# Delta-rule recurrence: multiplying by Z chunk by chunk instead of ahead of the loop

## The chip, the cores and the metric

The kernel runs on one core of a Trainium2 chip. A core has five engines with a queue each: TensorE (PE in the profile, with PEld for its weight loads), VectorE (DVE), ScalarE (ACT), GpSimd (POOL) and SyncE (SP). They work in parallel and wait for each other through semaphores. The metric is the device time of one execution in microseconds; the time given for a kernel is the median of its runs.

## What is computed

Two stages follow each other. The first is a recurrence over 768 tokens for 4 batches of 8 heads, with a state of 48 x 48 for each head; the second is a mixer over the 384 channels that the heads make together.

```python
k_n = k / (norm(k) + 1e-06)
for t in range(768):
    y[t]  = q[t] @ state
    v_old = k_n[t] @ state
    state = state + beta[t] * outer(k_n[t], v[t] - v_old)
x  = y of all heads, side by side                     # (4, 768, 384)
u  = x + (x.T @ U @ V).T                              # rank 32
out = u + relu(u @ w_ch1) @ w_ch2                     # 384 -> 1536 -> 384
```

## The kernel before

**Chunks.** The recurrence is not run token by token. The 768 tokens of a batch are cut into 12 chunks of 64 (`L`). Within a chunk the dependence of each token on those ahead of it is a triangular matrix, and the kernel inverts it, so that a chunk is a handful of products. Call the inverse Z, the keys of the chunk K, the (scaled) values v and the state ahead of the chunk S. What a chunk adds is z = Z v - (Z K) S; its outputs are the queries times S plus a masked product of queries and keys times z; the new state is S + K' z.

**Units.** Half a batch, six chunks, is a unit: units 0 and 1 belong to batch 0, units 2 and 3 to batch 1, and so on to unit 7. `grams` forms the products of keys and of queries and keys (L700), `norms` and `blocks` scale and invert (a long row of small DVE operations at L803 and L809, then joins of blocks on TensorE at L860, L874, L900, L903, L918 and L921, with ACT copies at L908, L927 and L939). The inverse of a unit lies in a region named `pg` or `zt`. The regions of two units alternate (`slot0`, `slot1`); the loads of unit n wait until the recurrence is through with unit n - 2 (L525).

**What is made ahead.** `prepare` (L1014) runs once for each half of a unit, three chunks. It makes Z K for all heads (24 products of 64 x 64, L1023) and Z v (24 products, L1034). Two ACT copies bring them back: Z K over the keys' region (L1042, 128 x 768 elements), Z v over the values (L1047, 128 x 576). It issues no DMA.

**The recurrence.** `recur` (L1055) has one turn for each chunk c. Step b multiplies Z K by the state (8 small products, L1072). A DVE operation subtracts that from Z v and gives z (L1085). Step s multiplies K by z (8 products, L1100) and a DVE operation adds it to the state (L1111). `outputs` (L975) makes the outputs in two steps of 8 products, y1 from the state (L983) and y2 from z (L997), and two ACT copies put them into `X` (L967). So the state goes round through two TensorE steps and two DVE operations in each chunk. Everything else in a chunk hangs beside that ring.

**The mixer.** When all chunks of a batch are done, `front` makes the low-rank part (L1393, L1412) and turns the result around (L1436). `wide` multiplies by `w_ch1` (L1497, ReLU on ACT at L1462) and `w_ch2` (L1617, gathered into `X` by DVE at L1537). The last batch uses another scheme for the first of these (L1296). The mixer of batch b runs while the recurrence of batch b + 1 does; that of the last batch has nothing beside it. The weights are converted by DVE and ACT operations at L1198, L1212, L1219 and L1226 in the first 150 us.

**Shapes on TensorE.** Mixer products use the whole array of 128 x 128 (L1497, L1617, L1436, L1296, and the transposes at L672). Those of the recurrence use it as four quarters of 64 x 64, and the joins at L900 to L921 as sixteen parts of 32 x 32.

**The order.** Every piece of work is a Python generator that yields what it does next. The string `ORDER` (L144 on) is a list written out in full: it says for each of some 2,260 steps which generator goes on. All engines' queues follow from it, and nothing reorders at run time; an engine waits at the head of its queue. Psum banks are taken in pairs: four pairs at first, three from the start of the mixer on.

Of the kernel before, what the change touches and what calls it, by code (L numbers as in the profile page):

```python
# [27 lines left out]
def kernel(  # L28
# [20 lines left out]
    nc = tc.nc  # L49
# [64 lines left out]
    def need(*keys):  # L114
        return [key for key in keys if key[1] >= 0]
# [29 lines left out]
    add_up b0 i0 f00: 573 585 613; add_up b0 i0 f03: 645 676 690; add_up b0 i1 f00: 795 797 800; add_up b0 i1 f03:  # L145
    818 819 824; add_up b0 i2 f00: 942 944 1042; add_up b0 i2 f03: 1023 1051 1071; add_up b1 i0 f00: 1161 1166 1186;
    add_up b1 i0 f03: 1189 1190 1191; add_up b1 i1 f00: 1309 1337 1363; add_up b1 i1 f03: 1357 1359 1368; add_up b1
    i2 f00: 1488 1493 1571; add_up b1 i2 f03: 1564 1572 1576; add_up b2 i0 f00: 1695 1717 1737; add_up b2 i0 f03:
    1728 1729 1730; add_up b2 i1 f00: 1888 1895 1906; add_up b2 i1 f03: 1886 1889 1901; add_up b2 i2 f00: 1992 2000
    2026; add_up b2 i2 f03: 2046 2047 2049; add_up b3 i0 f00: 2185 2186 2188; add_up b3 i0 f03: 2191 2192 2195;  # L150
    add_up b3 i1 f00: 2201 2202 2207; add_up b3 i1 f03: 2208 2209 2210; add_up b3 i2 f00: 2227 2228 2236; add_up b3
    i2 f03: 2224 2225 2229; blocks n0: 61 73 75 76 82 84 86 88 89 91 93 94 96 97 103 110 114 122; blocks n1: 143 157
    160 163 173 175 179 192 201 206 208 212 213 215 218 219 226 229; blocks n2: 479 496 501 502 508 512 513 514 515
    516 518 519 525 532 534 536 539 542; blocks n3: 704 720 721 729 730 733 739 741 761 765 769 771 772 773 778 779
    780 781 783 785 786 787 791 798 801 802 813 815 823 828 829 834 836 838; blocks n4: 971 982 985 987 989 996 1007
    1009 1012 1036 1038 1039 1040 1064 1074 1077 1082 1083 1087 1090 1107 1116 1119 1120 1122 1127 1129 1131 1132
    1133 1137 1138 1139 1140; blocks n5: 1168 1195 1198 1207 1218 1225 1227 1230 1231 1236 1241 1244 1249 1259 1269
    1271 1276 1278 1281 1286 1288 1291 1293 1294 1298 1311 1313 1314 1316 1323 1324 1332 1333 1351; blocks n6: 1510
    1523 1532 1541 1547 1558 1563 1566 1567 1568 1569 1596 1603 1612 1616 1617 1620 1622 1624 1645 1649 1653 1660
    1663 1665 1666 1671 1672 1673 1674 1675 1681 1684 1699; blocks n7: 1713 1724 1725 1739 1741 1744 1757 1762 1767  # L160
    1773 1775 1780 1782 1783 1800 1806 1807 1810 1817 1824 1829 1834 1837 1838 1849 1850 1856 1857 1860 1865 1866
    1867 1879 1881; both f0: 2149; both f1: 2105; both f2: 2147; both f3: 2123; both f4: 2111; both f5: 2184;
    channels b0 i0 e0: 546 547; channels b0 i0 e1: 549 550; channels b0 i0 e2: 552 553; channels b0 i0 e3: 567 574;
    channels b0 i0 e4: 588 591; channels b0 i0 e5: 604 633; channels b0 i1 e0: 768 776; channels b0 i1 e1: 777 788;
    channels b0 i1 e2: 790 792; channels b0 i1 e3: 799 803; channels b0 i1 e4: 806 807; channels b0 i1 e5: 808 814;
    channels b0 i2 e0: 898 899; channels b0 i2 e1: 907 912; channels b0 i2 e2: 935 936; channels b0 i2 e3: 950 959;
    channels b0 i2 e4: 965 969; channels b0 i2 e5: 995 1005; channels b1 i0 e0: 1118 1130; channels b1 i0 e1: 1136
    1148; channels b1 i0 e2: 1150 1151; channels b1 i0 e3: 1153 1155; channels b1 i0 e4: 1156 1158; channels b1 i0
    e5: 1159 1175; channels b1 i1 e0: 1297 1299; channels b1 i1 e1: 1300 1302; channels b1 i1 e2: 1304 1305; channels
    b1 i1 e3: 1306 1307; channels b1 i1 e4: 1326 1327; channels b1 i1 e5: 1342 1343; channels b1 i2 e0: 1430 1431;  # L170
    channels b1 i2 e1: 1432 1449; channels b1 i2 e2: 1450 1469; channels b1 i2 e3: 1470 1497; channels b1 i2 e4: 1498
    1501; channels b1 i2 e5: 1516 1530; channels b2 i0 e0: 1650 1654; channels b2 i0 e1: 1656 1669; channels b2 i0
    e2: 1686 1687; channels b2 i0 e3: 1689 1692; channels b2 i0 e4: 1697 1698; channels b2 i0 e5: 1700 1701; channels
    b2 i1 e0: 1808 1812; channels b2 i1 e1: 1813 1831; channels b2 i1 e2: 1833 1841; channels b2 i1 e3: 1843 1869;
    channels b2 i1 e4: 1871 1873; channels b2 i1 e5: 1874 1876; channels b2 i2 e0: 1950 1959; channels b2 i2 e1: 1960
    1961; channels b2 i2 e2: 1973 1979; channels b2 i2 e3: 1987 1999; channels b2 i2 e4: 2011 2027; channels b2 i2
    e5: 2033 2037; copies f0: 2127 2136; copies f1: 2082 2095; copies f2: 2129 2142; copies f3: 2086 2107; copies f4:
    2085 2103; copies f5: 2166 2168; cut f0 k0 to0: 2173; cut f0 k0 to1: 2169; cut f0 k1 to1: 2152; cut f1 k0 to0:
    2139; cut f1 k0 to1: 2106; cut f1 k1 to1: 2112; cut f2 k0 to0: 2153; cut f2 k0 to1: 2158; cut f2 k1 to1: 2163;
    cut f3 k0 to0: 2146; cut f3 k0 to1: 2154; cut f3 k1 to1: 2206; cut f4 k0 to0: 2171; cut f4 k0 to1: 2137; cut f4  # L180
    k1 to1: 2165; cut f5 k0 to0: 2181; cut f5 k0 to1: 2187; cut f5 k1 to1: 2194; diagonals n0 h0: 188 190 191 195 210
    222; diagonals n0 h1: 167 169 171 176 181 186; diagonals n1 h0: 312 315 319 336 343 353; diagonals n1 h1: 290 292
    303 338 349 358; diagonals n2 h0: 576 577 578 579 595 600; diagonals n2 h1: 632 646 665 670 705 707; diagonals n3
    h0: 854 855 860 865 870 873; diagonals n3 h1: 848 849 885 905 960 966; diagonals n4 h0: 1160 1162 1172 1197 1200
    1215; diagonals n4 h1: 1164 1192 1205 1211 1223 1226; diagonals n5 h0: 1356 1361 1365 1375 1402 1413; diagonals
    n5 h1: 1354 1380 1392 1419 1443 1444; diagonals n6 h0: 1708 1710 1711 1738 1745 1749; diagonals n6 h1: 1712 1723
    1726 1747 1753 1754; diagonals n7 h0: 1899 1905 1913 1931 1942 1945; diagonals n7 h1: 1892 1898 1911 1912 1918
    1957; first f0: 2160; first f1: 2097; first f2: 2135; first f3: 2138; first f4: 2092; first f5: 2180; front b0
    i0: 495 500 506 509 524 537; front b0 i1: 556 562 602 624; front b0 i2: 634 640 672 680; front b1 i0: 1055 1065
    1066 1078 1091 1111; front b1 i1: 1216 1224 1232 1237; front b1 i2: 1338 1348 1412 1425; front b2 i0: 1595 1599  # L190
    1605 1608 1623 1628; front b2 i1: 1633 1661 1702 1764; front b2 i2: 1801 1811 1835 1845; front b3 i0: 2041 2042
    2048 2050 2052 2054; front b3 i1: 2055 2061 2062 2067; front b3 i2: 2068 2070 2074 2076; gather b0 i0 h0 c0
    finalFalse: 671; gather b0 i0 h0 c0 finalTrue: 695; gather b0 i0 h0 c1 finalTrue: 756 1010; gather b0 i0 h1 c0
    finalFalse: 710; gather b0 i0 h1 c0 finalTrue: 757 805; gather b0 i0 h1 c1 finalFalse: 715; gather b0 i0 h1 c1
    finalTrue: 738; gather b0 i1 h0 c0 finalFalse: 820; gather b0 i1 h0 c0 finalTrue: 831; gather b0 i1 h0 c1
    finalTrue: 896 1061; gather b0 i1 h1 c0 finalFalse: 851; gather b0 i1 h1 c0 finalTrue: 881 1367; gather b0 i1 h1
    c1 finalFalse: 868; gather b0 i1 h1 c1 finalTrue: 867; gather b0 i2 h0 c0 finalFalse: 1017; gather b0 i2 h0 c0
    finalTrue: 1041; gather b0 i2 h0 c1 finalTrue: 1105 1185; gather b0 i2 h1 c0 finalFalse: 1079; gather b0 i2 h1 c0
    finalTrue: 1097 1163; gather b0 i2 h1 c1 finalFalse: 1084; gather b0 i2 h1 c1 finalTrue: 1086; gather b1 i0 h0 c0
    finalFalse: 1188; gather b1 i0 h0 c0 finalTrue: 1204; gather b1 i0 h0 c1 finalTrue: 1272 1778; gather b1 i0 h1 c0  # L200
    finalFalse: 1229; gather b1 i0 h1 c0 finalTrue: 1277 1591; gather b1 i0 h1 c1 finalFalse: 1238; gather b1 i0 h1
    c1 finalTrue: 1247; gather b1 i1 h0 c0 finalFalse: 1358; gather b1 i1 h0 c0 finalTrue: 1378; gather b1 i1 h0 c1
# [298 lines left out]

    TURNED = 3
    TURNED_K = 3
    SPLIT, QUARTERED = (0, 1), (2,)
    FIRST = dict(k1=11, q0=12, q1=13, z0=14, v0=15, z1=16, v1=17)
    FIRST = {(x[0], int(x[1])): y for x, y in FIRST.items()}

# [1188 lines left out]
```

## Time and profile before

| | |
|---|---|
| median of 3 runs | 599.51 us (597.67 to 601.25) |
| the profiled execution | 596.6 us, of which the profile's span is 594.9 us |
| DVE / ACT / POOL busy | 69% / 36% / 22% of the span |
| mean granted TensorE clock | 0.943 of full speed |
| Z K products, L1023 | 768 records, 16.8 us busy, last at 465.8 us |
| Z v products, L1034 | 768 records, 16.4 us busy, last at 466.7 us |
| step s, L1100 | 704 records, first at 61.0 us, last at 479.9 us |
| mixer, L1497 and L1617 | 150.1 us and, over three groups, 177.8 us busy |

A product is two records, since a 32-bit product is run as two instructions: a step of 8 products is "x16" in the trace and one of 24 is "x48". Lines of the trace give the start of a group, how long it lasted from the first start to the last end, the engine, the source line, what is written and read, and the shape; in brackets stands the idle time just before and who ended it. Groups on TensorE overlap, so the time that one takes from the next is read from start to start. In time, the program has four parts: until 60 us the first two units are loaded and inverted; until 108.5 us batch 0's recurrence runs, with no mixer work beside it; until 486 us the mixer of batches 0 to 2 and the recurrence of batches 1 to 3 share TensorE; the rest is the mixer of batch 3.

### The profile page before, as it was taken

The numbers are of one execution on the slowest core, as the hardware profiler recorded it, in microseconds if no ns is written. First come the engines' busy times: TensorE is split into PE (matmuls) and PEld (weight loads), VectorE is DVE, ScalarE is ACT, GpSimd is POOL, SyncE is SP. The second block draws the span as 40 slices with busy tenths as digits, with TensorE's granted clock in tenths as the row PEclk, the third lists the DMA queues.
The fourth block names the chain that finished last, engine by engine and source line by source line (L and its number), as shares of the span: only waits on it lengthen the run. The fifth ranks groups of instructions, "written<-read, shape, count | busy, mean of one in ns | idle before, by whom it ended". The sixth has DMA issues, their size and how long they took to land.

```text
span 594.9 us, 23426 instructions
## 1 busy us (share of the span) xinstructions
PE 559.7 (94%) x10428; PEld 481.6 (81%) x10428; DVE 409.3 (69%) x1011; ACT 216.8 (36%) x442; POOL 133.3 (22%) x229
## 2 busy tenths in 40 slices
PE   3778978899999999999999999999999999999997
PEld 3578977678988887989889887889899868656997
DVE  3888758899999458999884279998883235313542
ACT  1846475446322542035224341252243321335000
POOL 8122036116010724141205214520310000000000
PEclk9855556999999999999999999999999999999999
DMA  9981639714030415240402144420401000000000
GB/s 140 180 176 24 214 80 197 152 56 79 3 65 12 68 31 92 46 91 13 82 2 43 18 83 90 79 56 2 95 7 43 4 2 4 16 8 1 26 28 28
DMA packets 89445, 36.23 MB, mean 61 GB/s; under 512 B 75456, under 2 KB 87104, under 8 KB 89344
## 3 DMA queue, kind: packets, MB, share of 16 engines
q1 hardware_dynamic: 80800, 24.69, 20.7%
q0 software_dynamic: 6944, 9.74, 8.3%
q8 instruction: 82, 1.34, 1.0%
q10 hardware_dynamic: 1600, 0.30, 0.3%
q14 instruction: 19, 0.16, 0.1%
HBM read 29.98 MB, written 4.72 MB: 58 GB/s over the span
## 4 chain that ended last, share of the span: by engine, by line
PE 83%; DVE 11%; issue 2%; ACT 2%; DMA 1%; SPq 0%; DVEq 0%; ACTq 0%
PE P L1617 27%; PE P L1497 22%; PE P L1296 7%; PE P L700 4%; DVE xt L809 3%; DVE prod L803 3%; PE P L1072 2%; PE P L860 2%; PE P L874 2%; PE P L1023 2%; PE P L1034 2%; PE P L983 2%; PE P L997 2%; PE P L1100 2%; PE P L1412 2%
## 5 line engine op out<-in xcount | busy, mean ns | idle before, releaser
L1497 PE MATMUL P<-ut,w_sb 128*128 128x256 f32 x648 | 150.1, 385 | 1.5 <-ACT ut L1439 0.9
L1497 PEld LDWEIGHTS P<-ut,w_sb 128*128 128x128 f32 x648 | 119.9, 190 | 18.7 <-ACT ut L1439 1.1
L1617 PE MATMUL P<-w_sb,hs 128*128 128x192 f32 x540 | 96.7, 331 | 0.1
L1617 PEld LDWEIGHTS P<-w_sb,hs 128*128 128x128 f32 x540 | 87.2, 190 | 3.7 <-issue 1.2
L809 DVE TENSOR_TENSOR xt<-xt,prod 128x112 f32<-128x112 f32 (+21 forms) x200 | 64.6, 323 | 6.9
L803 DVE TENSOR_TENSOR prod<-gs,xt 128x112 f32<-128x112 f32 (+21 forms) x200 | 63.3, 316 | 3.5
L1537 DVE TENSOR_TENSOR X<-X,P 128x192 f32<-128x192 f32 x84 | 29.1, 349 | 49.8 <-PE P L1617 49.4
L1462 ACT ACTIVATE hs<-P 128x512 f32<-128x512 f32 x54 | 32.2, 598 | 77.5 <-PE P L1497 65.6
L967 ACT COPY X<-P 64x192 f32<-64x192 f32 x96 | 30.0, 313 | 66.3 <-PE P L997 63.4
L1617 PE MATMUL P<-w_sb,S 128*128 128x192 f32 x288 | 50.7, 330 | 0.0
L1617 PEld LDWEIGHTS P<-w_sb,S 128*128 128x128 f32 x288 | 46.6, 190 | 2.8 <-issue 1.8
L555 POOL DMA_DIRECT2D slot<-in_v_dram x32 | 21.1, 664 | 92.3 <-DVE prod L803 60.3
L1085 DVE TENSOR_TENSOR z<-slot,P 128x192 f32<-128x192 f32 x44 | 15.5, 352 | 30.8 <-PE P L1072 29.7
L541 POOL DMA_DIRECT2D slot<-in_q_dram x40 | 24.6, 621 | 46.9 <-DVE slot L747 33.3
L939 ACT COPY slot<-zz 32x384 f32<-32x384 f32 x64 | 32.4, 509 | 7.0 <-DVE zz L878 3.9
L700 PE MATMUL P<-slot 48*64 48x64 f32 x1536 | 30.9, 231 | 2.1 <-issue 1.4
L1296 PE MATMUL P<-slot,w_sb 128*128 128x384 f32 x96 | 32.9, 486 | 0.0
L700 PEld LDWEIGHTS P<-slot 48*64 48x64 f32 x1536 | 27.9, 144 | 5.6 <-issue 2.7
L946 POOL MEMSET slot<- 32x384 f32 x32 | 13.3, 421 | 84.2 <-PE P L903 63.4
L1617 PE MATMUL P<-w_sb,slot 128*128 128x192 f32 x180 | 30.4, 327 | 0.9 <-DVE X L1537 0.9
L555 POOL DMA_DIRECT2D slot<-in_k_dram x44 | 29.4, 670 | 8.3 <-PE P L1100 7.6
L1617 PEld LDWEIGHTS P<-w_sb,slot 128*128 128x128 f32 x180 | 29.3, 190 | 1.7 <-DVE X L1537 1.5
(153 smaller groups left out, 901.4 us busy)
## 6 DMA issues: line engine op xcount, KB each, us to landing
out_dram<-X SPq DMA_DIRECT2D x22, 192.0 KB, 2.7
w_sb<-in_moe_w_ch_dram SPq DMA_DIRECT2D x10, 384.0 KB, 5.6
slot<-in_k_dram SPq DMA_DIRECT2D x48, 72.0 KB, 3.9
slot<-in_k_dram POOLq DMA_DIRECT2D x44, 72.0 KB, 3.8
slot<-in_v_dram SPq DMA_DIRECT2D x32, 72.0 KB, 3.7
slot<-in_v_dram POOLq DMA_DIRECT2D x32, 72.0 KB, 3.5
X<-in_moe_w_ch_dram SPq DMA_DIRECT2D x6, 384.0 KB, 6.1
wide<-in_moe_w_ch_dram SPq DMA_DIRECT2D x6, 384.0 KB, 5.0
```

The source lines that it names most:

```text
L541: queue.dma_start(out=blocked(n)[quarter(y % 4), j, g, :, 0:w], in_=src[b, 4 * g + 2 * j + par, hf * UC * L : (hf + 1) * UC * L, BK * low ...
L555: queue.dma_start(out=t[half(1 - g if name == "z" else g), :, to, 0:D], in_=src[b, 4 * g + s, hf * UC * L : (hf + 1) * UC * L, :].rearrang ...
L700: nc.tensor.matmul(p_g[half(g ^ (par * i)), par, c], kq[rows, c, j, 0, half(g)], kq[rows, c, j, i, half(g)], start=True, stop=True,)
L803: nc.vector.tensor_tensor(out=prod, in0=gb[:, :, j : j + 1, j + 1 :].to_broadcast([128, split, m, w]), in1=xb[:, :, 0:m, j : j + 1].to_bro ...
L809: nc.vector.tensor_tensor(out=xb[:, :, 0:m, j + 1 :], in0=xb[:, :, 0:m, j + 1 :], in1=prod, op=ALU.subtract,)
L939: nc.scalar.copy(pg[quarter(i), :, at, :, a : a + BK], cut(zc, h)[quarter(i)].rearrange("p r (c j) t -> p r c j t", j=2),)
L967: nc.scalar.copy(x[half(c % 2), c // 2, 4 * D * g : 4 * D * (g + 1)].rearrange("p (j r d) -> p r j d", r=2, d=D), states(p_y)[half(g)],)
L1296: nc.tensor.matmul(to, w, t, start=start, stop=stop, skip_group_check=True)
L1462: nc.scalar.activation(hs[:, fs[0] : fs[1] + 1 : fs[1] - fs[0]], p_f, ACTF.Relu)
L1497: nc.tensor.matmul(p_f[:, x], w(x, t), ut[:, t], start=(t == 0), stop=(t == KT - 1))
L1537: nc.vector.tensor_tensor(out=to, in0=to, in1=p, op=ALU.add)
L1617: nc.tensor.matmul(to, of[0], of[1], start=of[2], stop=of[3], skip_group_check=True)
```

## The change

For units 1 to 7 `prepare` ends without making anything. The recurrence multiplies the keys themselves (not Z K) by the state, subtracts that from v (not Z v), in place in the values' region, and then multiplies by Z: one more step of 8 products for each chunk, followed by a ScalarE copy into `z`. In the new kernel these are L1101 and L1111, step b is L1076 (its psum halves swap for these units), the subtraction is L1091 and step s is L1121. Unit 0 stays as it was. The wait for the outputs of chunk c - 3, which protects `z`, moves from the subtraction to the copy.

`ORDER` is new as a whole. It has fewer `prepare` steps and more `recur` steps, and everything else is in another order too.

```diff
     ORDER = """
...
     """
+    DIRECT = (1,2,3,4,5,6,7)
...
             yield need(("upper", n, h), ("diagonal", n, h), ("grams", n), ("scaled", n), *landed("k", n, 0), *landed("k", n))
+            if n in DIRECT:
+                emitted(("ready", n, h))
+                return
             cs = range(3 * h, 3 * h + 3)
...
-            kn, kq, _, _, _, vn, _, kz = units[n]
+            kn, kq, zt, _, _, vn, _, kz = units[n]
+            direct = n in DIRECT
...
-            else:
+            if c > 0:
                 xb = yield op("pe", 0.23, "Q", take="pair", words=32, flow=0.16)
                 p_b = pair(xb)[:, :, 0 : 2 * D]
                 for j, par, g in heads:
                     nc.tensor.matmul(
-                        states(p_b)[half(g ^ par), par, j],
+                        states(p_b)[half(g ^ (0 if direct else par)), par, j],
                         kq[half(par, D), cu, j, 0, half(g)],
                         states(s_old)[half(par, D), g, j],
...
-                yield need(("y", b, c - 3)) if c > 2 else []
+                yield need(("y", b, c - 3)) if c > 2 and not direct else []
                 yield op("dve", dve(192), give=[("pair", xb)])
-                z = zs[c] = small.tile([128, 4, D], FP32, name="z", bufs=3)
+                z = vn[:, cu]
+                if not direct:
+                    z = zs[c] = small.tile([128, 4, D], FP32, name="z", bufs=3)
                 nc.vector.tensor_tensor(
                     out=z.rearrange("p (r j) d -> p r (j d)", r=2),
                     in0=vn[:, cu].rearrange("p (r j) d -> p r (j d)", r=2),
                     in1=p_b,
                     op=ALU.subtract,
                 )
+            if direct:
+                xz = yield op("pe", 0.23, "Q", take="pair", words=32, flow=0.16)
+                p_z = pair(xz)[:, :, 0 : 2 * D]
+                for j, par, g in heads:
+                    nc.tensor.matmul(
+                        states(p_z)[half(g ^ par), par, j],
+                        zt[half(g), par, cu, j],
+                        vn[half(g), cu, 2 * par + j],
+                        start=True,
+                        stop=True,
+                    )
+                yield need(("y", b, c - 3)) if c > 2 else []
+                yield op("act", act(192), give=[("pair", xz)], rush=True)
+                z = zs[c] = small.tile([128, 4, D], FP32, name="z", bufs=3)
+                nc.scalar.copy(z.rearrange("p (r j) d -> p r (j d)", r=2), p_z)
             emitted(("z", b, c))
```

## The prediction

> **What bounds the kernel now.** I read the page's first two parts, then the busy time by stretches of the span, then the list of groups, then the timeline of TensorE in two places.
>
> ```profile
> PE 559.7 (94%) x10428; PEld 481.6 (81%) x10428; DVE 409.3 (69%) x1011; ACT 216.8 (36%) x442; POOL 133.3 (22%) x229
> PE   3778978899999999999999999999999999999997
> PEclk9855556999999999999999999999999999999999
> ```
>
> ```profile
> 60.00:108.50 48.50, 41.46 (x1382) 37.96 (x1380) 34.89 (x65) 28.52 (x60) 14.72 (x25) 0.62 0.67 172
> 108.50:150.00 41.50, 38.71 (x1022) 31.11 (x1023) 39.24 (x86) 20.92 (x37) 14.29 (x23) 1.00 0.40 77
> 150.00:486.00 336.00, 333.82 (x6430) 292.12 (x6424) 251.47 (x647) 114.20 (x241) 80.86 (x136) 1.00 0.23 45
> ```
>
> The columns of the second fence are the stretch, its length, the busy time of PE, PEld, DVE, ACT and POOL, the granted clock, the DMA share and GB/s. From 150 to 486 us TensorE is busy for 333.8 of 336 us: there a step taken off TensorE is time won, as long as the order keeps other work ready, and ACT (34%) has room. From 60 to 108.5 us it is different: PE is at 85%, the clock at 0.62, and there is no mixer work to fill a gap, so the ring of batch 0's recurrence sets the pace. What these two places gain and lose is the prediction; after 486 us nothing changes.
>
> **What is removed and added on TensorE.**
>
> ```profile
> L1072 PE MATMUL P<-s,slot 48*64 48x48 f32 x704 | 21.4, 239 | 1.0 <-DVE s L1111 0.8 <-ACT slot L720 0.2
> L1023 PE MATMUL P<-slot 64*64 64x64 f32 x768 | 16.8, 238 | 0.9 <-DVE s L1111 0.5 <-ACT slot L939 0.3
> L1034 PE MATMUL P<-slot 64*64 64x48 f32 x768 | 16.4, 231 | 0.6 <-issue 0.6
> L1042 ACT COPY slot<-P 128x768 f32<-128x768 f32 x16 | 12.8, 800 | 30.5 <-PE P L1023 30.5
> L1047 ACT COPY slot<-P 128x576 f32<-128x576 f32 x16 | 10.3, 642 | 0.7 <-PE P L1034 0.7
> L908 ACT COPY zz<-P 128x192 f32<-128x192 f32 x16 | 4.7, 319 | 8.1 <-PE P L903 7.9 <-ACT zz L865 0.2
> ```
>
> Fourteen of the sixteen halves lose a step of 24 products (L1023) and one of 24 that comes back as three steps of 8 (L1034). ACT loses 14 x (0.80 + 0.64) = 20.2 us and gains 42 copies of 128 x 192, which the row of L908 prices at 0.32: 13.4 us. It gets 6.7 us lighter. DVE does what it did.
>
> The prices come from starts in the timeline of PE:
>
> ```profile
> 469.07 1.56 PE L1497 MATMUL P<-ut,w_sb 128*128 128x256 f32 x6
> 470.56 0.45 PE L1072 MATMUL P<-s,slot 48*64 48x48 f32 x16
> 470.83 0.41 PE L983 MATMUL P<-s,slot 48*64 48x48 f32 x16
> 471.06 0.41 PE L997 MATMUL P<-z,slot 64*64 64x48 f32 x16
> 471.48 0.40 PE L1100 MATMUL P<-z,slot 64*48 64x48 f32 x16
> 471.81 1.56 PE L1497 MATMUL P<-ut,w_sb 128*128 128x256 f32 x6
> ```
>
> A step of 8 takes 0.23 to 0.27 from the next (0.235 over many); one of 24 takes 0.70 (L1023 at 283.29, L1034 at 284.00). Three mixer products that stand alone take 1.49 (469.07 to 470.56), and six take 2.79, so the three alone pay 1.49 - 1.30 = 0.19 for coming into and leaving the whole-array shape. A quarter-array stretch pays some 0.14 beyond its steps (one step alone: 0.38).
>
> I counted the stretches and steps between the low-rank steps (L1393) of batches 0 and 3 in the order of PE instructions of the two built programs:
>
> - steps of 24: 46 before, 22 after; steps of 8: 135 and 171
> - whole-array stretches: 69 and 80; quarter-array: 56 and 74; stretches of joins: 15 and 19
>
> So: -24 x 0.70 = -16.8; +36 x 0.235 = +8.5; +11 x 0.19 = +2.1; +22 x 0.14 = +3.1. Work from 108.5 to 486 us: **-3.1 us**. The new order spends more than half of what the removed product saves on changes of the array's shape and on the third step.
>
> **The wait that is added.** A turn of the ring had two links and has three. A link is from the start of a step to the start of the one that needs it: L1072 at 470.56 starts the subtraction at 471.07 (0.51), that takes 0.35, and the next step can go 0.05 later: 0.92 us, against 0.235 of PE's own. The new link goes over ACT: 0.48 (L997 at 471.06 to its copy at 471.54) + 0.32 + 0.05 = 0.85. PE must have some 0.65 of other work in each link; while it has not, every step behind waits too, the mixer's among them. Between L1072 and L1100 above lie two steps, and 0.17 us is lost. Walking the PE order of both programs with these prices, I added up how far each link between 108.5 and 486 us falls short: before, 10 of 63 links are short, by 2.4 us in all; after, 19 of 99, by 5.5 us. That is **+3.1 us**. The stalls of this kind in the trace add up to about the same (near 231, 360 and 416 us, 2.5 us in all), so I take the sum as it is. The copy also queues behind ACT's other work, ReLU above all (L1462, 0.60 us each): 8 of the 36 copies directly follow a ReLU in ACT's order, which at 34% busy times half of 0.6 each is 0.8 us at most; a covered link hides its share, and I take **+0.3**. What waits behind such a copy on ACT is the copy of outputs (L967) and the ReLU, and on them hang psum pairs that step b takes.
>
> The unit's inverse must now last until its sixth chunk. That costs nothing: the next unit's loads into the slot already wait for the recurrence's end (L525), and no DMA moves to another queue or gains a wait of its own.
>
> **The opening, 60 to 108.5 us.** Here unit 1's six chunks get the longer ring, and its preparation goes.
>
> ```profile
> 82.71 0.64 PE L1072 MATMUL P<-s,slot 48*64 48x48 f32 x16
> 83.13 1.37 PE L997 MATMUL P<-z,slot 64*64 64x48 f32 x32
> 84.29 1.52 PE L1023 MATMUL P<-slot 64*64 64x64 f32 x48
> 85.59 0.55 PE L1100 MATMUL P<-z,slot 64*48 64x48 f32 x16
> 85.91 1.20 PE L1034 MATMUL P<-slot 64*64 64x48 f32 x48
> 87.65 0.93 PE L1023 MATMUL P<-slot 64*64 64x64 f32 x48 [0.54 <-DVE s L1111]
> 88.40 0.40 PE L1072 MATMUL P<-s,slot 48*64 48x48 f32 x16
> ```
>
> Chunk 5's step s stands behind L1023, and chunk 6's step b waits for both ACT copies. That turn takes 5.7 us (82.71 to 88.40); turns without preparation take 2.1 to 3.3 (88.40, 91.08, 93.21, 96.53, 98.98), and I take 2.9. So the removal wins **2.8**. The added link of chunks 6 to 9 and 11 has no cover, and that of chunk 10 lies under unit 2's transposes and products (100.0 to 104.5, on PE at that place in both orders). Six more transposes (0.87 us) move from behind L1393 to ahead of it, which changes no sum. A link costs 0.9 at full clock and, at the half clock of most of this stretch, 1.1 (L997 at 76.96 and L1072 at 75.93 reach their reader 0.7 to 0.75 later). I take 1.0 x 5 = **+5.0**. The copy stands in ACT's queue among weight conversions (L1198, 0.92) in a stretch where ACT is 60% busy: 5 x 0.24 = **+1.2**. Together **+3.4**. Bounds: if DVE's conversions already hold the ring back as long as the link adds, it is -2.8; with all six links bare and two of them behind a whole conversion, 6 x 1.1 + 1.8 - 1.0 = +7.4. I stay between, since DVE was 72% busy here and delayed some turns, not all. From 108.5 us on PE is the bound, so a late start is passed on to the end.
>
> **Sum.** -3.1 + 3.1 + 0.3 + 3.4 = +3.7 us on the profiled execution: 596.6 + 3.7 = 600.3. It lies 2.9 below the median of the runs shown, and so does the forecast: 599.5 + 3.7 = **603.2 us**.
>
> **Rivals.**
> - *The saved product comes through* (**faster**): the stalls of the middle are covered (ACT is lighter by 6.7 us, and a link that is short lacks 0.29 us on average) and the opening comes out even. -3.1 to -5.5 (if before's own 2.4 go too): 594 to 596. For it speaks the 99% of PE between 150 and 486 us; against it, that the new order cuts mixer work into stretches of three products and still leaves links short.
> - *It cancels* (**no change**): the opening costs 0 to 2. 597 to 602.
> - *The clock falls* (much **slower**): the granted clock was 0.53 from 60 to 88 us, where PE was busy 89%, and 1.00 from 108.5 to 150 us, at 93%. If batch 1's first chunks take PE below some 88% there, the half clock could stay for 10 us or more of mixer work, at about twice its time: +10, 613. The trace never shows it once mixer products run, so I give it little. The Trainium skill ("TensorE: Matmul & The Clock Gate", Part 1) speaks against the change here: it says that the default is the throttled clock and that an idle window of about 3.4 us brings it back. By that rule alone the added stalls, each under 1 us, would not trip it; the trace's 0.53 at 89% busy shows that many small products with short gaps do not earn the full clock either.
> - *The product was hidden*, so that its removal wins nothing: with PE busy for 333.8 of 336 us I give it no chance of its own.
>
> **How the numbers follow.** What a measurement of this kernel can tell from no change is about 0.5%, 3 us. My forecast of slower has 0.45, the falling clock 0.05, cancelling 0.25 and the saved product 0.25. The forecast's own range is 602.5 to 608 (opening up to +7.4 with the middle at 0 to +1). The range that is to hold 8 in 10 reaches into the other cases, from 595.5 to 608.5.
>
> **What would show it.** L1023 and L1034 with 96 records each; L1101 with 672 records, L1111 with 42 copies of 0.32; ACT's busy time near 210 us. First L1393 (L1414 in the new kernel) at 111 to 113 us instead of 108.55, with unit 1's turns at 3.5 to 4 us: the opening's step. Time from there to batch 3's low-rank step near 377 us, as before: the middle's. If that distance is shorter by 3 us or more, my count of stalls was wrong; if the opening is no later, the ring was not what set its pace. A granted clock of 0.5 after 115 us would be the third rival.

## The result, and the profile after

The changed kernel takes 602.82 us, median of 18 runs (601.11 to 605.21), beside 599.75 us for the kernel before (595.18 to 602.75, 18 runs on the same chip): a ratio of 1.0057 [1.0036, 1.0079]. It is about 3 us slower; 603.2 was forecast. Its profiled execution took 605.2 us, with a span of 603.5.

From the page of the changed kernel: the busy times, two rows of the span in 40 slices (each digit a tenth), and the group of the new copy.

```profile
PE 563.9 (93%) x9756; PEld 478.8 (79%) x9756; DVE 410.3 (68%) x1011; ACT 212.0 (35%) x456; POOL 133.4 (22%) x229
...
PE   4677888899999998999999999999999999999997
...
PEclk9656555899999999999999999999989999999999
...
L1111 ACT COPY z<-P 128x192 f32<-128x192 f32 x42 | 13.4, 319 | 56.4 <-PE P L1101 53.2
```

TensorE runs 672 fewer matmul records (10428 to 9756), and yet it is busy 4.2 us longer. Nearly all of that lies in the opening, where the granted clock is lower: 0.56 from 60 us on, against 0.62 before. From 108.55 us on before and from 114.63 us on after, up to the low-rank step of batch 3, it is busy for 372.2 and 372.4 us. The row PEclk shows why the second figure is not smaller: an 8 among the nines near three quarters of the span, which the kernel before does not have. Busy time by stretches shows both (columns as before: stretch, length, busy PE, PEld, DVE, ACT, POOL, granted clock, DMA share, GB/s):

```profile
60.00:114.63 54.63, 47.04 (x1361) 42.40 (x1353) 40.35 (x74) 31.86 (x68) 8.26 (x14) 0.56 0.55 136
114.63:150.00 35.37, 33.90 (x857) 27.13 (x857) 33.76 (x74) 15.92 (x29) 17.67 (x29) 1.00 0.54 102
150.00:440.00 290.00, 286.37 (x4950) 247.07 (x4948) 235.60 (x610) 94.70 (x210) 79.86 (x133) 1.00 0.27 51
440.00:448.90 8.90, 7.45 (x247) 6.69 (x247) 5.93 (x11) 5.12 (x12) 4.19 (x8) 1.00 0.12 29
448.90:452.30 3.40, 3.40 (x13) 3.40 (x12) 0.43 (x1) 1.47 (x4) 0.00 (x0) 0.50 0.09 22
452.30:494.22 41.92, 41.24 (x788) 33.18 (x786) 11.84 (x35) 11.92 (x32) 0.00 (x0) 1.00 0.04 12
```

For 3.4 us, from 448.9 on, TensorE gets half its clock, in the middle of mixer work. The other difference is in the first line: the opening ends at 114.63 us instead of 108.55. Part of that is work that only moved: six more transposes (L672), 0.7 to 0.9 us at full clock, stand ahead of the low-rank step in the new order.

To say where time goes I use four marks: T0 to T3 are the starts of the low-rank step of batches 0 to 3 (L1393 before, L1414 after). Until T0 lies the opening, from T0 to T3 the shared work; after T3 the kernels take 109.2 and 109.3 us. Since one execution differs from the next, all are listed; "half clock" is what the granted clock shows after 115 us.

| execution | T0 | T0 to T3 | half clock |
|---|---|---|---|
| before, the profile above | 108.55 | 377.2 | none |
| rep_before (the kernel before again) | 105.85 | 378.6 | none |
| rep_before2 (once more) | 109.43 | 381.6 | 234.8 to 241.6 |
| after | 114.63 | 379.6 | 448.9 to 452.3 |
| rep_after (the changed kernel again) | 110.04 | 380.6 | 444.8 to 448.2 |

The two profiles lie 8.6 us apart, which is not the effect: the profile of before is one of its quick executions, that of after one of the slow ones of its kernel.

### The profile page after: what moved, and what is told of

It reads as the page before. It is cut to its first block, busy times and chain, and to the rows that moved or that the text cites. A ratio compares the mean times of both kernels' runs of the same rounds, so it can differ in the third digit from the quotient of the medians.

```text
span 603.5 us, 22066 instructions
## 1 busy us (share of the span) xinstructions
PE 563.9 (93%) x9756; PEld 478.8 (79%) x9756; DVE 410.3 (68%) x1011; ACT 212.0 (35%) x456; POOL 133.4 (22%) x229
## 4 chain that ended last, share of the span: by engine, by line
PE 89%; DVE 5%; issue 2%; ACT 2%; DMA 1%; DVEq 0%; POOL 0%; ACTq 0%
PE P L1638 29%; PE P L1518 24%; PE P L1317 7%; PE P L700 4%; PE P L1076 3%; PE P L1101 3%; PE P L1121 2%; PE P L983 2%; PE P L997 2%; PE P L874 2%; PE P L672 2%; PE P L860 2%; PE P L1414 1%; PE P L1457 1%; PE P L1433 1%
## 5 line engine op out<-in xcount | busy, mean ns | idle before, releaser
L1518 PE MATMUL P<-ut,w_sb 128*128 128x256 f32 x648 | 154.4, 388 | 0.9 <-ACT ut L1460 0.9
L1518 PEld LDWEIGHTS P<-ut,w_sb 128*128 128x128 f32 x648 | 118.6, 190 | 18.3 <-ACT ut L1460 1.1
L1638 PE MATMUL P<-w_sb,hs 128*128 128x192 f32 x540 | 97.5, 333 | 0.0
L1638 PEld LDWEIGHTS P<-w_sb,hs 128*128 128x128 f32 x540 | 88.6, 192 | 3.1 <-issue 1.8
L1638 PE MATMUL P<-w_sb,S 128*128 128x192 f32 x288 | 51.5, 331 | 0.0
L1638 PEld LDWEIGHTS P<-w_sb,S 128*128 128x128 f32 x288 | 47.2, 191 | 2.3 <-DVE prod L803 1.2
L1111 ACT COPY z<-P 128x192 f32<-128x192 f32 x42 | 13.4, 319 | 56.4 <-PE P L1101 53.2
L700 PE MATMUL P<-slot 48*64 48x64 f32 x1536 | 32.9, 239 | 0.3 <-DVE slot L684 0.2
L700 PEld LDWEIGHTS P<-slot 48*64 48x64 f32 x1536 | 29.5, 151 | 3.9 <-issue 1.4
L1132 DVE TENSOR_TENSOR s<-s,P 128x192 f32<-128x192 f32 x40 | 14.1, 352 | 26.9 <-PE P L1121 22.6
L1638 PE MATMUL P<-w_sb,slot 128*128 128x192 f32 x180 | 30.7, 328 | 0.9 <-DVE X L1558 0.9
L1638 PEld LDWEIGHTS P<-w_sb,slot 128*128 128x128 f32 x180 | 29.3, 190 | 2.1 <-DVE X L1558 1.8
```

Source lines behind the costliest of these rows:

```text
L700: nc.tensor.matmul(p_g[half(g ^ (par * i)), par, c], kq[rows, c, j, 0, half(g)], kq[rows, c, j, i, half(g)], start=True, stop=True,)
L1518: nc.tensor.matmul(p_f[:, x], w(x, t), ut[:, t], start=(t == 0), stop=(t == KT - 1))
L1638: nc.tensor.matmul(to, of[0], of[1], start=of[2], stop=of[3], skip_group_check=True)
```

## The experiments

Two theories stood against each other. One: the change costs what its steps cost (the longer ring in the opening), and the middle comes out even. The other: what is lost is lost in the middle, to the half clock near 445 us and what brings it on.

**Does the half clock come back?** Another execution of each kernel, unchanged.

> The changed kernel, once more, for a second profile. Theory: the turns of unit 1's ring again take 3.5 to 4 us, the low-rank step comes at 111 to 115 us, and without a drop of the clock batch 3's low-rank step follows 376 to 377 us later, as in the kernel before. Rival (the clock): the half clock shows again after 115 us, and the distance is 379 us or more.

> The kernel before, once more, for a second profile. If the two profiles at hand stand for their kernels, the first low-rank step comes at 108 to 110 us and batch 3's 377 us after it, with no half clock after 115 us. If executions differ by themselves as much as the two profiles do (8.6 us of span, against 3.1 us between the medians), the first low-rank step comes later than 111 us, or the distance is another by 2 us or more.

rep_after took 601.64 us, rep_before 595.27. T0 came earlier than expected in both. The half clock is in rep_after at the same place in the order, and so it is in every other kernel below that keeps this part of the new order unchanged. It belongs to the order there and is not an accident of one execution. T0 of rep_after is 4.6 us earlier than in the profile of after with the same order: single values of T0 are worth no more than that. It goes with the granted clock: until T0, TensorE was at half clock for 85.3 us in after and for 71.7 us in rep_after.

**What brings it on.** The timeline of TensorE in the changed kernel, ahead of the slow window (start, length, engine, line, tiles; idle time before it in brackets):

```profile
444.87 0.45 PE L983 MATMUL P<-s,slot 48*64 48x48 f32 x16
445.13 0.36 PE L1121 MATMUL P<-z,slot 64*48 64x48 f32 x16
...
445.70 0.22 PE L918 MATMUL P<-zz 32*32 32x32 f32 x2
447.38 0.21 PE L921 MATMUL P<-zz 32*32 32x32 f32 x1 [1.45 <-issue]
...
447.63 0.45 PE L1076 MATMUL P<-s,slot 48*64 48x48 f32 x16
447.89 0.41 PE L997 MATMUL P<-z,slot 64*64 64x48 f32 x16
448.24 3.59 PE L1638 MATMUL P<-w_sb,hs 128*128 128x192 f32 x12
451.62 2.46 PE L1638 MATMUL P<-w_sb,S 128*128 128x192 f32 x12
```

Three stretches of small products follow each other without any mixer work: joins of unit 7 (L900 and L903, 443.84 to 444.87), two steps of 8, joins again (L918 and L921). In the middle of the last, TensorE stands for 1.45 us, and the profile names no releaser ("issue"): it waited for nothing that the profile shows. Then 24 mixer records take 448.24 to 454.02, 5.8 us, where 12 take 2.1 elsewhere (2 x 2.05 = 4.1): 1.7 us too long, for 3.4 us at half speed. Idle and half clock are some 3.2 us together.

no_drop moves one step of the mixer, six products of L1638, eleven places forward, so that it stands between the two stretches of joins. Nothing else in the order differs, nothing in the code.

```diff
-narrow b2 i1 e0: 1899 1935
+narrow b2 i1 e0: 1899 1924
```

> The changed kernel with one step moved: in batch 2, six mixer products (L1638) go between the two stretches of joins of unit 7 that stand close together, where the trace shows TensorE idle for 1.4 to 1.5 us and then 3.4 us at half clock. Theory: that idle time and the half clock disappear, one stretch more costs 0.33, and the kernel is 2.5 to 3.5 us faster than the changed kernel. Rival (the half clock comes from something else, or the lost time reappears): within 1 us of the changed kernel.

It took 599.96 us (12 runs), 1.0018 [0.9992, 1.0044] of the kernel before. The same place in its timeline (its lines are three higher, so L1641 is L1638):

```profile
441.46 0.45 PE L986 MATMUL P<-s,slot 48*64 48x48 f32 x16
441.73 0.36 PE L1124 MATMUL P<-z,slot 64*48 64x48 f32 x16
442.01 2.22 PE L1641 MATMUL P<-w_sb,hs 128*128 128x192 f32 x12
444.16 0.21 PE L921 MATMUL P<-zz 32*32 32x32 f32 x1
...
444.71 0.45 PE L1079 MATMUL P<-s,slot 48*64 48x48 f32 x16
444.98 0.41 PE L1000 MATMUL P<-z,slot 64*64 64x48 f32 x16
445.32 2.22 PE L1641 MATMUL P<-w_sb,S 128*128 128x192 f32 x12
```

The idle is gone, and with it the half clock: T2 to T3 falls from 123.8 us in both executions of the changed kernel to 120.7, and T0 to T3 to 377.1. All executions agree, those without a profile too. Each has a span and a mean granted clock on record, and twice the missing share of the clock, times the span, is its time at half clock: 80.4 us on average in the 18 runs of the changed kernel and 77.3 us in the 12 of no_drop, about one window of 3.4 us less. By the medians this one move is worth 602.82 - 599.96 = 2.9 us; by the ratios, 0.0039 x 599.75 = 2.3 us. That is most of what the change lost: all the rest of the change together costs 0.0018 x 599.75 = 1.1 us (-0.5 to 2.6), which can't be told from nothing. Whether the hole or the sparse small products alone would have brought the half clock is not told apart, since the move takes both away.

**What the idle on "issue" is.** The profile's list of DMA queues has one of the kind "instruction". Its packets (number, MB, share of the DMA engines), for the whole changed kernel and then from 445 to 446 us:

```profile
q8 instruction: 76, 1.25, 0.9%
```

```profile
q8 instruction: 1, 0.02, 5.9%
```

Every packet has 16 KB, and there is one for about 257 of TensorE's 19,512 records, weight loads counted (82 packets and 20,856 records in the kernel before, one for 254). The one that starts at 445.01 lands at 445.96 us, and the hole ends 1.42 us later. After 40 us the twelve traces hold 26 idle stretches of TensorE on "issue" of 0.9 us or more. Each of them ends 1.2 to 1.6 us behind the landing of such a packet, and each falls at the same place, number 193 or 194, in a group of 256 of TensorE's records, counted from its first. So TensorE stands there because its next block of instructions has not come. The joins of L900 and L903 use up 193 records in 1.03 us; a dozen mixer records with their weight loads take 2.04 us. In no_drop TensorE still has 60 records ahead of the same place when the packet lands, the rest of the moved mixer step among them, and it passes without a hole. What decides when a packet is asked for stays open.

**The step that was added.** no_z leaves the multiplication by Z out for units 1 to 7 (the product and its copy), in the new order otherwise; what the recurrence subtracts goes on as z.

```diff
-                xz = yield op("pe", 0.23, "Q", take="pair", words=32, flow=0.16)
...
-                nc.scalar.copy(z.rearrange("p (r j) d -> p r (j d)", r=2), p_z)
+                zs[c] = vn[:, cu]
```

> The changed kernel without the Z step and its copy in units 1 to 7 (z is left as v - K S, so the inverse is not applied in these units); all else in the changed order. Theory: the opening wins 5 links of 1.0 and the copies' queueing, 5 to 6 us; the middle wins 36 x 0.235 = 8.5 us of steps, 6 lone stretches x 0.33 = 2.0 and the 3 us of stalls: 13 to 14. In all 16 to 20 us. Rival (the step hides beside other work and only the links count): 6 to 9 us.

It took 595.14 us (10 runs), 0.9961 [0.9928, 0.9994]: 7.7 us less than the changed kernel by the medians, 5.8 by the ratios (0.0096), and not 16 to 20. T1 to T3 gave 7.9 (251.8 to 243.9), T0 to T1 1.7 (127.8 to 126.1), and the opening next to nothing: T0 is at 112.9, as late as with the step. Its waits of TensorE from 86 to 113 us (line, who ended the wait: us in all, times, longest):

```profile
PE P L1074 <- DVE s L1118: 4.1, 5, 1.6
PE P L981 <- ACT X L965: 1.5, 1, 1.5
```

With the link away, the ring waits for DVE's update of the state (L1118 here, L1132 in the changed kernel; L1074 is step b and L981 the outputs' first step) for 4.1 us, up to 1.6 at a time, where the changed kernel waits 2.4 with 0.5 as the longest; and for ACT. DVE and ACT have conversions of weights in their queues there. The order was laid out for the long ring, and the same places with a short one probably meet other work ahead of them. So leaving the step out in a fixed order doesn't measure what the step costs in the opening. A window of half clock remains in the middle here as well, from 441.4 to 444.8.

**The opening alone.** u1_ahead gives unit 1 its preparation back within the new order; u1_only does the reverse, the order of before with unit 1 alone on the new path, its Z step and copy directly behind the subtraction.

```diff
-    DIRECT = (1,2,3,4,5,6,7)
+    DIRECT = (2,3,4,5,6,7)
```

```diff
-    DIRECT = (1,2,3,4,5,6,7)
+    DIRECT = (1,)
```

> The changed kernel with unit 1 prepared ahead again (L1023 and L1034 back for it, its Z steps and copies gone); the order is the changed one, with the preparation put behind the same recurrence steps as in the kernel before. Theory (the opening is what was lost): unit 1's turns fall back to 2.1 to 3.3 us, the low-rank step comes 3 to 4 us earlier than in the changed kernel, and the time falls by as much, to within 1.5 us of the kernel before. Rival (the middle is what was lost): the time stays within 1 us of the changed kernel.

> The kernel before, in its own order, with unit 1 alone multiplied by Z in the recurrence: its eight preparation steps are gone, and each Z step with its copy stands right behind the subtraction. Theory A (the prediction's: the longer ring of unit 1 costs the opening): 3.4 us slower than the kernel before, low-rank step at 109 to 112 us. Theory B (the changed order of the opening costs it, and the link is about paid for by the preparation that goes): within 1 us of the kernel before, low-rank step at 105 to 109 us.

Both missed. u1_ahead took 607.32 us (5 runs), 1.0164 [1.0137, 1.0190], 4.5 us slower than the changed kernel by the medians and 6.4 by the ratios, with T0 at 114.7; the half clock near 450 us is there too. Unit 1's turns, without the added link, took 15.6 us from chunk 6's step b to chunk 10's, since the preparation now stood among them and two holes on issue, of 1.6 and 1.3 us, fell there. u1_only took 612.81 us (6 runs), 1.0244 [1.0210, 1.0277]. Its turns from chunk 6 to 10 took 3.4 to 3.7 us, about 0.9 above the 2.6 that they take on average in the profile of before. But T0 came at 116.3, and T0 to T1 took 135.7 us, some 7 more than before. The waits of TensorE from 90 to 125 us:

```profile
PE P L986 <- issue: 2.9, 1, 2.9
PE P L1079 <- DVE s L1135: 1.0, 2, 0.5
PE P L1104 <- DVE slot L1094: 0.5, 1, 0.5
```

A hole of 2.9 us of the same kind as above, and half clock from 111.6 to 118.4 and from 128.6 to 132.1. Taking or adding steps also moves the ends of the instruction blocks to other work, so neither gives a clean price for the change in the opening.

**The opening of before, the middle of after.** splice_move has the order of before up to T0, with unit 1 prepared ahead, then that of the changed kernel with the moved step of no_drop. late4 does the same with the cut at T1, with units 4 to 7 on the new path.

```diff
-    DIRECT = (1,2,3,4,5,6,7)
+    DIRECT = (2, 3, 4, 5, 6, 7)
```

```diff
-    DIRECT = (1,2,3,4,5,6,7)
+    DIRECT = (4, 5, 6, 7)
```

> The order of the kernel before up to the low-rank step of batch 0, with units 0 and 1 prepared ahead, then the changed order with units 2 to 7 multiplied by Z in the recurrence, and the move of the run before. Theory (the opening's order is where most was lost, the rest of the change wins about 1 us): low-rank step at 105 to 109 us, batch 3's 376 to 377.5 us later, 0.5 to 2 us faster than the kernel before. Rival (units 2 to 7 lose by themselves): 1 us slower than the kernel before or more.

> The order of the kernel before up to the low-rank step of batch 1, with units 0 to 3 prepared ahead; from there the changed order, with units 4 to 7 multiplied by Z in the recurrence and the six mixer products moved as in the run no_drop. Theory: the opening and batch 0's mixer are those of the kernel before, from batch 1's low-rank step to batch 3's it takes 248.6 us as in no_drop where the kernel before takes 249.8, and the kernel is 1 us faster than the one before, about what can be told. Rival (the two orders don't fit where they are joined): 1 us slower or more.

splice_move took 599.89 us (12 runs), 1.0015 [0.9989, 1.0041]; late4 600.14 (12 runs), 1.0023 [0.9991, 1.0055]. Neither can be told from the kernel before. splice_move's T0 to T3 is 377.1, that of no_drop to 0.1 us, so the middle repeats; its T0 is 110.7, no better than no_drop's 110.6, in part since transposes of unit 2 (L672) came to lie ahead of it at the joint of the orders. late4 lost a window of half clock at 236.0 to 239.4, and T0 to T3 was 381.7. Up to T1, at 243.1 us, late4 has the order of before, so this loss and its T0, 110.1, are those of the order of before in one more execution. From T1 to T3 it takes 248.8 us, as no_drop does (248.6), beside 250.0 and 249.7 before.

**The product that was removed.** no_zk is the kernel before without the product Z K and its copy for units 1 to 7, and nothing put in its place: the recurrence uses K where Z K belongs.

```diff
-            x = yield op("pe", 0.70, "Q", take="pair", words=96, flow=0.64)
+            if n == 0:
+                x = yield op("pe", 0.70, "Q", take="pair", words=96, flow=0.64)
...
-            yield op("act", act(768), give=[("pair", x)])
+            if n == 0:
+                yield op("act", act(768), give=[("pair", x)])
```

> The kernel before without the product Z K and its copy for units 1 to 7 (the keys stay unmultiplied there), order unchanged: what is removed, with nothing added. Theory: 12 steps of 0.70 us in the middle and two in the opening: 8.4 + 1.3 to 2.8, so 9.5 to 11 us faster than the kernel before, at 588 to 590 where it is at 599. Rival (the steps fill time that would be idle anyway): 0 to 4 us.

It took 593.95 us (10 runs), 0.9908 [0.9879, 0.9937]: 5.5 us less by the ratio and by the medians (599.46 to 593.95). T1 to T3 fell to 246.2, from 250.0 in the profile of before and 249.7 in rep_before. But T0 to T1 rose to 131.5, from 127.2 and 128.9. The same stretches in no_zk:

```profile
106.81:132.80 25.99, 22.20 (x522) 16.11 (x522) 22.44 (x58) 8.93 (x15) 4.25 (x7) 1.00 0.34 76
132.80:139.60 6.80, 6.23 (x26) 5.01 (x26) 4.74 (x8) 2.25 (x4) 3.54 (x6) 0.50 0.44 66
```

There is an idle of 2.1 us on issue (at L861), from 131.3 to 133.4 us, and 6.8 us at half clock from 132.8 on. The time saved is neither the 9.5 to 11 us of the theory nor the 0 to 4 of the rival: the product was not hidden, but part of its gain was given back there. Whether the hole came because the stretch got thinner or because the ends of the instruction blocks moved is not told apart.

**Is it the change that loses the clock?** One more execution of the kernel before.

> The kernel before, a third profile. If its two profiles at hand lie low by chance (596.6 and 595.3 us against a median of 599.5), this one shows where the rest comes from: a low-rank step later than 108.6 us, or idle time of TensorE without a releaser in the profile. If the profiles are not by chance, low-rank step at 105.8 to 108.6 us and 377 to 378.6 us to batch 3's.

It took 601.88 us, 6.6 more than rep_before, and lost the clock from 234.8 to 241.6 us. Its timeline and its stretches there:

```profile
233.74 0.44 PE L997 MATMUL P<-z,slot 64*64 64x48 f32 x15 [0.24 <-DVE z L1085]
235.86 0.34 PE L997 MATMUL P<-z,slot 64*64 64x48 f32 x1 [1.68 <-issue]
```

```profile
228.00:234.80 6.80, 5.13 (x194) 4.05 (x185) 5.46 (x19) 2.48 (x7) 6.78 (x11) 1.00 0.78 163
234.80:241.60 6.80, 5.74 (x25) 4.33 (x29) 3.16 (x9) 0.63 (x2) 0.40 (x2) 0.50 0.55 104
```

Same order, same instructions as in the profile of before, where this place passes at full clock. So the kernel before loses windows in some of its executions (late4 shows one more, at the same place), and that is probably a part of why its runs spread from 594.6 to 603.4 us. The changed kernel adds a place that showed it in both of its executions profiled.

## Why the prediction was right, and where its terms were off

The forecast, +3.7 for 603.2 us, was met: the medians differ by 3.1 us, the ratio makes 3.4. By its mechanism it was met only in part. It put nearly the whole loss into the opening (+3.4 of +3.7); no_drop shows 2.3 to 2.9 us lost behind one place in the middle, and about 1 us for all the rest. That the sum came out so near is luck.

**Work and stalls of the middle: -3.1 + 3.1 + 0.3.** Without the half clock T0 to T3 is 377.1, beside 377.2 and 378.6 before, and some 0.7 to 0.9 us of it moved ahead of T0: the sum of about nothing held within 1 us. Its parts were both smaller. TensorE's busy time from T0 to T3 is 370.4 us in no_drop and 372.2 in the profile of before: -1.8 where -3.1 was priced. The waits of TensorE in the changed kernel, from 115 to 486 us:

```profile
PE P L921 <- issue: 1.5, 1, 1.5
PE P L983 <- DVE s L1132: 1.2, 2, 0.6
PE P L1101 <- DVE slot L1091: 0.9, 3, 0.3
...
PE P L1121 <- ACT z L1111: 0.5, 2, 0.3
...
PE P L997 <- ACT z L1111: 0.2, 1, 0.2
```

The four that belong to the ring add up to 2.8 us. Before, the ring's are 1.1 (L983 0.6 and L997 0.5, from 108 to 486 us). So the added stalls are some 1.7 to 2, where 5.5 - 2.4 = 3.1 was counted.

**The clock rival.** This is the step that failed: the prediction gave a half clock once mixer products run 5 in 100 and one size, +10 us, at batch 1's first chunks. It came in both executions of the changed kernel that were profiled, at another place (unit 7's joins), for one window of 3.4 us, and with the idle ahead of it cost about 3. The mechanism named was right in so far as a stretch in which TensorE is too little busy came ahead of it; the place, the price and the chance were not. The prediction looked for that stretch among the waits of the ring. What its count of stalls left out is the idle of 1.45 us in which TensorE waits for its next instructions, at the end of a block that three stretches of small products had used up.

**The opening: -2.8 + 5.0 + 1.2 = +3.4.** T0 was expected at 111 to 113; it is 114.6 and 110.0, and 110.6 in no_drop, which has the same order up to there. None of the three lies in that range, but their mean does: 111.7, against 107.9 for the three executions of before (+3.8), or 108.5 with late4 (+3.2). Of that, 0.7 to 0.9 is the six transposes that moved. It doesn't show a loss of 3.4 us through the ring. The granted clock is a rival: where the time at half clock until T0 is the same 71.7 us, T0 is 109.4 and 110.1 in the order of before (rep_before2, late4) and 110.0 and 110.6 in the new one (rep_after, no_drop). And with the whole of the new opening in it, no_drop is only 1.1 us slower than the kernel before. Whether the longer ring brings the half clock with it, the runs don't show. Its terms: chunk 5's turn took 5.7 us and takes 2.8 (b at 83.6 and 86.4): the 2.8 won is 2.9. A turn with three links, chunk 7's, in the changed kernel's timeline:

```profile
89.99 0.68 PE L1076 MATMUL P<-s,slot 48*64 48x48 f32 x16 [0.53 <-DVE s L1132]
90.44 0.64 PE L983 MATMUL P<-s,slot 48*64 48x48 f32 x16
91.21 0.68 PE L1101 MATMUL P<-slot 64*64 64x48 f32 x16
91.67 0.64 PE L997 MATMUL P<-z,slot 64*64 64x48 f32 x16
92.35 0.57 PE L1121 MATMUL P<-z,slot 64*48 64x48 f32 x16
93.47 0.68 PE L1076 MATMUL P<-s,slot 48*64 48x48 f32 x16 [0.55 <-DVE s L1132]
```

Three links of 1.22, 1.14 and 1.12 us, 3.5 for the turn. From chunk 6's step b to chunk 10's it is 14.7 and 14.1 us (after, rep_after), beside 10.6 and 10.4 (before, rep_before): 3.5 to 4.3 us for four links, or about 1.0 each, as priced. There is no room in that for the +1.2 of ACT's queue. But the same turns of the order of before took 12.5 us in rep_before2 and 13.7 in late4, with 3.0 and 3.5 us of idle on issue among them, so in those executions the longer ring cost 0.4 to 2.2 us there. Chunk 10's link was probably not hidden in full: its step s comes 6.4 to 6.9 us after step b, beside 5.7 to 6.2 in the three executions of before and 6.7 in late4. The bound of +7.4 holds a term of -1.0 for which the prediction gives no row. And one loss was not in the sum: the new order keeps TensorE waiting before 60 us already. The waits from 40 to 64 us, after and then before:

```profile
PE P L918 <- ACT zz L908: 2.6, 2, 2.0
PE P L1026 <- issue: 1.5, 1, 1.5
PE P L997 <- issue: 1.1, 1, 1.1
```

```profile
PE P L918 <- ACT zz L908: 1.5, 2, 0.9
PE P L700 <- DVE slot L731: 0.7, 1, 0.7
```

5.2 us against 2.2: the first step s is at 63.4, 61.9 and 61.7 us in the new order, 61.1, 58.7 and 58.8 in the old. Of the 5.2 us, 2.6 are on issue, TensorE waiting for instructions. The prediction took the opening to begin at 60 us in both. Part of this is won back in batch 0's first turns.

**ACT and the records.** 672 records of L1101, 42 copies of 0.319 us and 212.0 us of ACT, as said (4.8 less than before, 6.7 forecast).

**The saved product and cancelling.** Without the half clock the kernel would have come out even with before within the measurement: no_drop, 1.0018. No version made here that leaves nothing out beats the kernel before, and whether an order made anew for this change could, was not tried.

Three things stay open: what one link costs in the opening with all else alike, what decides when a block of instructions is fetched, and what share of the later T0 is the ring, what the order ahead of it and what the granted clock.

## What to carry to other kernels

When an edit comes with a new order, price the order as well: look for stretches in which one engine runs nothing but tiny instructions, since there its supply of instructions can break, and the clock with it. Idle without a releaser that ends just behind a packet of the instruction queue is of this kind. A stretch of large products put between two such stretches won back most of what this edit had lost. To remove one step from a fixed schedule is a poor measure of the step, for the work behind it was placed for the longer chain, and the instruction blocks end elsewhere.

## What the runs showed of the hardware

- Half clock came in windows of 3.4 or 6.8 us, each of those after 115 us directly behind 3.4 us in which TensorE was busy for 67% or less. In the changed kernel:

```profile
442.10:445.50 3.40, 3.40 (x148) 3.08 (x149) 1.28 (x3) 3.12 (x8) 0.91 (x3) 1.00 0.02 5
445.50:448.90 3.40, 1.95 (x84) 1.74 (x85) 2.58 (x6) 1.41 (x4) 3.29 (x6) 1.00 0.30 72
```

  1.95 of 3.4 is 57%; it was 1.98 in rep_after, 1.81 in rep_before2, 1.78 in late4, 1.88 in no_zk and 2.27 in no_z. u1_only's second window, from 128.6 on, came behind only 0.7. But from 117.8 to 121.2 us the changed kernel was busy for 2.16 of 3.4 and kept its clock, so the share alone does not decide it. The Trainium skill ("TensorE: Matmul & The Clock Gate", Part 1) says that an idle window of some 3.4 us throttles the clock, and that the window runs freely. The length of 3.4 us agrees with these traces, and so does the free run: within each trace all changes of the granted clock lie on one grid of 3.41 us. That the window must be idle does not, since holes of 1.45 and 1.68 us were enough. The phase on that grid doesn't explain the stretch at 118 us: the window given, and one from 130.8 to 134.2 in no_z with 1.8 us busy, lie on the grid of their traces.
- Idle on "issue", with no releaser in the profile, came in holes of 0.4 to 2.9 us in the places named here, and those of 0.9 us or more after 40 us all end 1.2 to 1.6 us after a 16 KB packet of the instruction queue landed. They differ between executions of the same kernel: at one place in the order of before there were 1.68 us in rep_before2 (at 234 us), 0.84 in late4, 0.43 in rep_before and none in the profile of before.
